# A wide layer's third quarter of weights decoded later, and the memory of the change lent to expert weights: attention, soft experts and a wide layer on one core

## The chip, the cores and the metric

The kernel runs on one core of a Trainium2 chip. TensorE (PE) multiplies matrices, VectorE (DVE) and ScalarE (ACT) work on the rest, GpSimd (POOL) has a few additions, and SyncE (SP) only issues transfers between device memory and the core's memory. The metric is the time of one execution on the device in microseconds (us).

## The reference

Three stages follow one another: a thresholded softmax attention, a layer of soft experts, and a wide layer. x has 2304 rows of 512.

```
scores = q @ k.T / sqrt(64)                       # 4 batches, 8 heads, 576 x 576
scores = where(scores >= rowmax(scores) - tau, scores, -1e9)
x = (softmax(scores) @ v)                         # heads side by side: 2304 x 512

logits = x @ phi                                  # 32 slots, 4 for each of 8 experts
slot_input = softmax(logits, over tokens).T @ x   # 32 x 512
slot_out[e] = relu(slot_input[e] @ w1[e]) @ w2[e] # w1 512x1024, w2 1024x512
x = softmax(logits, over slots) @ slot_out        # 2304 x 512

h = x @ w_in                                      # w_in 512 x 2048, in float64
out = (h * sigmoid(1.702 * h)) @ w_out            # w_out 2048 x 512, in float64
```

## The kernel before

**Attention** runs in 16 units (4 batches by 4 pairs of heads) of 9 tiles each. The order of the instructions is written out: a table PLAN gives each step a place within the 9 tiles of a unit, the steps of all units are sorted by these keys, and while they are issued `InOrder.on` keeps each engine's instructions in the order in which they stand in the program.

**Decoding.** w_in and w_out come as float64, that is as two 32-bit words per number. A piece is loaded as `raw` (SP, line 147), and the helper at line 134 records its work: ACT makes `y<-raw`; DVE makes `y<-y`, `top<-raw,y`, `y<-top`, `y<-raw,y`. For w_in one POOL addition of top and y gives the weights in f32. For w_out ACT casts top to `wo_h`, and DVE makes `top<-top,wo_h` and `wo_l<-top,y`, so that the weights are kept as a high and a low part. The buffers raw, y and top are each 3 deep in the wide layer (2 in attention).

The first WA columns of w_in are decoded in attention, in pieces of 128 x 256 (24 of them before: two in each of units 0 to 11) into the tiles `wi`. The columns behind WA are decoded in the wide layer, in pieces of 128 x 512 called "late" (4 before). The list `stream` of the wide layer has 9 pieces of w_out, the late pieces, then 7 of w_out.

**Experts.** w1 and w2 of 8 experts make 64 quarters of 512 KB. They are loaded into rings of buffers (a, b, c, ...), each of which takes memory that another use has left; some are loaded slowly in attention (`slow_load`), the others after it. Layer 1 is at line 1034, layer 2 at line 1076; a buffer of ring m, a or b is filled again as soon as an expert's work on it is over.

**Wide layer.** After the experts, slots times w_in gives `ws` (32 slots by 2048 hiddens, in pieces a, b, c, d of 384 or 512 columns behind a first one of 128). Since a sum of 4 products of 32 rows is taken side by side, a piece goes through PE (`w_ps`, line 1207), a copy to memory on ACT (`wqs`, line 1212), PE again (`w_ps<-wqs,sel`, line 1215), and from there into ws on ACT and DVE. Then 48 steps follow: 3 groups of 6 token tiles by 8 blocks of 128 hiddens, for the first half of the hiddens, and the same for the second half. A step makes `h_ps` (line 1249) in a part of 512 and one of 256 tokens, `sg` and `gh` on ACT (lines 1254, 1236), `gw` on DVE (line 1238), and 18 products `y_ps` (lines 1275 to 1277) with the weights of the step's hiddens. Sums of the first half are parked in memory (`part`, line 1285). Beside a step goes, in the first 5 steps and in the odd ones after them, the decoding of the next piece of the stream. SEQ and TAIL give the places of the pieces of ws: c is made at steps 4 and 5, d at 18 and 19 (the first of each pair is w_ps and wqs, the second the rest). In PSUM, the w_ps of a late piece of ws takes the one buffer, tag h0, in which the h_ps of 512 tokens is made too. In this stage Tile's scheduler sets the order on each engine from the program's order and from what depends on what; each engine works through its own list in order.

Of the kernel before, what the change touches and what calls it, by code (L numbers as in the profile page):

```python
# [19 lines left out]
def kernel(  # L20
# [14 lines left out]
    nc = tc.nc  # L35
# [19 lines left out]
    WA = 1536  # L55
# [3 lines left out]
    SEQ, TAIL, LATE = "wabhwawbhh", {4: "c", 5: "c", 18: "d", 19: "d"}, 9  # L59
# [15 lines left out]
    wi = [ring_a.tile([P, 2, WA], F32, tag="wi", name=f"wi{i}", bufs=2) for i in range(2)]  # L75


    order = [(1, 0), (1, 1), (1, 2), (2, 0), (1, 3), (2, 1)] + [(1, e) for e in range(4, E)]
    order += [(2, e) for e in range(2, E)]
    quarters = [(layer, e, j) for layer, e in order for j in range(4)]  # L80
    rings, ring_ctx, w_rows = {"a": ring_a}, {}, {}
# [3 lines left out]
    def load_quarters(ring, n, spread=False):  # L85
# [3 lines left out]
        while i < n and quarters:  # L89
# [8 lines left out]
            if spread:  # L98
                slow.append(io)
            else:  # L100
                nc.sync.dma_start(**io)
# [42 lines left out]
    first = [True]  # L144

    def load(**io):
        ins = nc.sync.dma_start(**io)  # L147
        if first[0]:
            tc.keep_in_program_order(ins)
# [42 lines left out]
    def w_in_piece(pool, j):  # L192
# [4 lines left out]
                out=wi[kc // 2][:, kc % 2, cols], in0=top, in1=rest  # L197
# [21 lines left out]
    def late_piece(pool, j, wl):  # L219
        n, kc = divmod(j, KC)  # L220
        cols = slice(n * DM, (n + 1) * DM)
        return decoding(
            pool, ("late", j), DM,
            lambda top, rest: po.tensor_add(out=wl[kc // 2][:, kc % 2, cols], in0=top, in1=rest),
# [20 lines left out]
    def attention():  # L245
# [3 lines left out]
        def psum(name, bufs):  # L249
# [3 lines left out]
        st, rows, sums, late_p2, early_p2, exp_e, odd_units, even_units, loads, weights_in = (  # L253
            ExitStack() for _ in range(10)
# [7 lines left out]
        pp = [pool(late_p2, f"pp{i}", 1, RIGHT) for i in range(2)]  # L262
        pp.append(pool(early_p2, "pp2", 1, RIGHT))
# [229 lines left out]
        def across(u, half):  # L493
# [8 lines left out]
            def after():  # L502
                row = l_row[u, half] = ptp.tile([P, 2 * P + R], F32, tag="l_row", name="l_row", bufs=2)
# [9 lines left out]
        def products_of(u, half):  # L513
            if (u, half) not in pt:
                n = 2 * P + half * R
                pt[u, half] = ptp.tile([P, 2, C, n], F32, tag=f"pt{half}", name="pt")
                ptr[u, half] = ptp.tile([P, n], F32, tag=f"ptr{half}", name="ptr")
# [365 lines left out]
        def unit(u):  # L883
# [49 lines left out]
            if u >= 4:  # L933
                for t in (7, 8):
# [39 lines left out]
        at(max(ends[f"DA{d}"] for d in range(2)) + 0.0001, swap, weights_in, "b", 4)  # L974
# [3 lines left out]
        freed("Q K R", floor, lambda: swap(loads, "c", 4))  # L978
        before = {n: TPU * (NU - 2) + max(PLAN[n][0:2]) for n in pairs.split()}
        floor[0] = max([floor[0]] + list(before.values())) + 0.0001  # L980
        at(floor[0], swap, even_units, "d", 2)
# [410 lines left out]
```

## Time and profile before

| | |
|---|---|
| time, median of 3 | 600.97 us (600.52 to 601.35) |
| profiled execution | 601.18 us, of which its span is 599.0 |
| PE | 582.7 us busy, 97% of the span |
| DVE | 400.5 us, 67% |
| ACT | 374.1 us, 62% |
| POOL | 140.9 us, 24% |
| bytes read from device memory | 64.55 MB |

Times of rows are from the start of the span. Attention lasts to about 320 us, the experts to about 363, the wide layer to the end. A busy share is an average over stages that have different limits. Where a row ends in square brackets, they hold the idle time of the engine just before it, and what ended it. Busy times of neighbouring instructions on one engine may overlap by some hundredths of a us.

### The profile page before, as it was taken

What the parts mean: (1) busy time and instruction counts of PE and PEld (TensorE: products, weight loads), DVE (VectorE), ACT (ScalarE), POOL (GpSimd) and SP (SyncE); (2) the same over time, 40 slices, a digit from 0 to 9 for tenths busy, and PEclk for the clock granted to TensorE, in tenths of its full rate; (3) what the DMA queues carried; (4) which work ended last, traced back from release to release, by engine and by line L of the source; (5) the groups of instructions that cost most, each with busy time, mean ns of one, the idle gap of its engine ahead of it and who ended that gap; (6) DMA issues with size and microseconds to landing.
All of it is one profiled execution on the core that took longest, in us unless ns stands there. A gap on an engine that the chain in (4) does not pass through costs nothing.

```text
span 599.0 us, 10535 instructions
## 1 busy us (share of the span) xinstructions
PE 582.7 (97%) x3712; PEld 414.1 (69%) x3712; DVE 400.5 (67%) x998; ACT 374.1 (62%) x804; POOL 140.9 (24%) x310
## 2 busy tenths in 40 slices
PE   7999999999999999999998998999999999999996
PEld 5666767667677676766765424778887788888884
DVE  3889899798997998878682435999981211512422
ACT  4788888788888798878861106767673354334330
POOL 1445445554455644222220100003000000000000
PEclk9899999999999999999999999999999999999999
DMA  7524054362542633420249993333310000200203
GB/s 223 136 74 124 21 161 144 88 180 92 161 143 62 172 125 80 138 75 24 87 150 369 410 409 144 134 120 130 138 37 0 1 0 1 105 1 0 106 0 106
DMA packets 63011, 69.94 MB, mean 117 GB/s; under 512 B 42736, under 2 KB 46832, under 8 KB 62960
## 3 DMA queue, kind: packets, MB, share of 16 engines
q1 hardware_dynamic: 62960, 69.28, 35.6%
q8 instruction: 29, 0.48, 0.3%
q14 instruction: 22, 0.18, 0.1%
HBM read 64.55 MB, written 4.72 MB: 116 GB/s over the span
## 4 chain that ended last, share of the span: by engine, by line
PE 87%; DVE 5%; DMA 3%; ACT 1%; SPq 1%; issue 1%; POOL 0%; DVEq 0%; POOLq 0%; ACTq 0%
PE s_ps L134 13%; PE o_ps L134 13%; PE y_ps L1275 11%; PE y_ps L1277 11%; PE y_ps L1276 11%; PE pt_ps L134 10%; PE r_ps L134 4%; PE h_ps L1249 3%; DVE p L134 3%; DMA w_c<-in_moe_w_dram 2%; PE acc L1034 2%; PE q_t L134 1%; SPq L147 1%; PE x_ps L134 1%; PE lg_ps L134 1%
## 5 line engine op out<-in xcount | busy, mean ns | idle before, releaser
L134 DVE SCALAR_TENSOR_TENSOR p<-p,th,e_sb 128x576 f32<-128x576 f32 x144 | 118.0, 841 | 13.5 <-ACT e_sb L134 11.4
L134 ACT ACTIVATE e_sb<-p,mn 128x576 f32<-128x576 f32 x144 | 110.7, 781 | 21.2 <-DVE p L134 20.3
L1275 PE MATMUL y_ps<-wo_h,gh 128*128 128x512 f32 x288 | 113.8, 396 | 0.0
L1276 PE MATMUL y_ps<-wo_l,gh 128*128 128x512 f32 x288 | 113.5, 394 | 0.0
L1277 PE MATMUL y_ps<-wo_h,gw 128*128 128x512 f32 x288 | 113.3, 395 | 0.0
L1238 DVE TENSOR_TENSOR gw<-sg,gh 128x768 fp32r<-128x768 f32 (+2 forms) x49 | 45.9, 939 | 91.9 <-ACT gh L1236 91.7
L134 DVE TENSOR_SCALAR_CACHE_REDUCE p<-s_ps 128x576 f32<-128x576 f32 x120 | 87.1, 751 | 10.3 <-PE pt_ps L134 6.6
L134 ACT COPY pt<-pt_ps 128x512 f32<-128x512 f32 x142 | 82.2, 586 | 17.8 <-PE pt_ps L134 17.1
L1254 ACT ACTIVATE sg<-h_ps 128x512 f32<-128x512 f32 (+1 forms) x96 | 42.5, 491 | 78.4 <-PE h_ps L1249 78.4
L134 PE MATMUL pt_ps<-ident,p 128*128 128x128 f32 x580 | 88.3, 280 | 0.5 <-DVE p L134 0.3
L134 PE MATMUL s_ps<-kx,qx 64*128 64x288 f32 x512 | 86.1, 438 | 2.2 <-DVE p L134 1.7
L134 PEld LDWEIGHTS pt_ps<-ident,p 128*128 128x128 f32 x580 | 65.3, 142 | 23.8 <-ACT ptr L134 5.4
L134 PE MATMUL o_ps<-pt,vn 128*64 128x320 f32 (+1 forms) x512 | 69.6, 412 | 0.3 <-ACT pt L134 0.3
L134 PEld LDWEIGHTS s_ps<-kx,qx 64*128 64x128 f32 x512 | 47.6, 189 | 25.0 <-issue 7.0
L1275 PEld LDWEIGHTS y_ps<-wo_h,gh 128*128 128x128 f32 x288 | 53.9, 187 | 14.1 <-ACT gh L1236 0.8
L1277 PEld LDWEIGHTS y_ps<-wo_h,gw 128*128 128x128 f32 x288 | 53.8, 187 | 13.5 <-DVE gw L1238 0.2
L1276 PEld LDWEIGHTS y_ps<-wo_l,gh 128*128 128x128 f32 x288 | 54.0, 187 | 11.2
L134 PEld LDWEIGHTS o_ps<-pt,vn 128*64 128x64 f32 x512 | 33.7, 136 | 31.0 <-issue 10.6
L134 POOL TENSOR_TENSOR th<-mn,few 128x1 f32<-128x1 f32 x144 | 38.7, 278 | 68.3 <-DVE p L134 63.4
L1236 ACT CAST gh<-sg 128x768 fp32r<-128x768 f32 (+2 forms) x49 | 40.2, 823 | 1.2
L134 POOL COPY lw<-l 128x256 f32<-128x256 f32 (+1 forms) x48 | 21.7, 472 | 34.8 <-PE r_ps L134 17.2
L134 ACT ACTIVATE y<-raw 128x256 f32<-128x256 f32 (+1 forms) x44 | 24.3, 551 | 8.9 <-DMA raw<-in_moe_w_out_dram 6.5
(189 smaller groups left out, 743.3 us busy)
## 6 DMA issues: line engine op xcount, KB each, us to landing
raw<-in_moe_w_out_dram SPq DMA_DIRECT2D x16, 512.0 KB, 3.3
raw<-in_moe_w_in_dram SPq DMA_DIRECT2D x24, 256.0 KB, 2.9
w_a<-in_moe_w_dram SPq DMA_DIRECT2D x12, 512.0 KB, 4.4
w_a<-in_moe_w_dram SPq DMA_DIRECT2D x6, 1024.0 KB, 13.8
qn<-in_q_dram SPq DMA_DIRECT2D x16, 256.0 KB, 3.7
kn<-in_k_dram SPq DMA_DIRECT2D x16, 256.0 KB, 4.0
vn<-in_v_dram SPq DMA_DIRECT2D x16, 256.0 KB, 2.9
w_m<-in_moe_w_dram SPq DMA_DIRECT2D x6, 512.0 KB, 5.0
```

The costliest lines, as they stand in the source:

```text
L134: ins = call(*args, **kw)
L147: ins = nc.sync.dma_start(**io)
L1034: nc.tensor.matmul(acc1[j][kc * NS:(kc + 1) * NS, :], s_in[kc // 2][:, kc % 2, e * NS:(e + 1) * NS], w_rows[1, e, kc][:, j * 512:(j + 1) * ...
L1236: nc.scalar.copy(out=gh[:, a], in_=sg[:, a])
L1238: nc.vector.tensor_sub(out=gw[:, a], in0=sg[:, a], in1=gh[:, a].bitcast(F32))
L1249: nc.tensor.matmul(ps, ws[:, f * P:(f + 1) * P], cs[:, t:t + n, :].rearrange("p t n -> p (t n)"), start=True, stop=True,)
L1254: nc.scalar.activation(out=part, in_=ps, func=AF.Gelu_apprx_sigmoid)
L1275: nc.tensor.matmul(ys[t], gh[:, tk], w_h, start=first, stop=False)
L1276: nc.tensor.matmul(ys[t], gh[:, tk], w_l, start=False, stop=False)
L1277: nc.tensor.matmul(ys[t], gw[:, tk], w_h, start=False, stop=last)
```

## The change

WA falls from 1536 to 1024. Pieces of w_in decoded in attention become 16 (units 0 to 7), late pieces 8. The tile wi takes 16 KB of a partition where two took 24, and what is left becomes two more buffers of ring c. The four quarters of ring c were one load of 2 MB; now six are loaded slowly, within units 9 and 10. The transposed weights of a unit's first half move from the pool ptp into one of their own, ptp0, which is given to ring p (2 quarters) before the last second half is over. Ring n (1 quarter) takes the memory of the loads of Q and K. Rings d and i hold one quarter less. Loads in attention are now chained to each other in the order of the table. From unit 3 on three slow loads stand in a unit, where two stood from unit 4 on. In layer 2 ring m is filled again, ring c no longer. In the wide layer piece c of ws moves from steps 4 and 5 to 13 and 14, d to 19 and 20, and steps 8, 12, 16 and 20 carry a piece of the stream where they had none. The parked sums of the first half lie in wi, ring m and ring k.

```diff
     PW = 256
-    WA = 1536
+    WA = 1024
     ES = NS + SE
     QSCALE = 1.0 / float(D) ** 0.5
     IN_ORDER = True
-    SEQ, TAIL, LATE = "wabhwawbhh", {4: "c", 5: "c", 18: "d", 19: "d"}, 9
+    SEQ, TAIL, LATE = "wabhwawbhh", {13: "c", 14: "c", 19: "d", 20: "d"}, 9
+    EXTRA = (8, 12, 16, 20)
     AHEAD = 3
...
     y_acc = const.tile([P, DM], F32, name="y_acc")
-    wi = [ring_a.tile([P, 2, WA], F32, tag="wi", name=f"wi{i}", bufs=2) for i in range(2)]
-
-
-    order = [(1, 0), (1, 1), (1, 2), (2, 0), (1, 3), (2, 1)] + [(1, e) for e in range(4, E)]
-    order += [(2, e) for e in range(2, E)]
+    wi = ring_a.tile([P, KC, WA], F32, tag="wi", name="wi", bufs=1)
+
+
+    order = [(1, 0), (1, 1), (1, 2), (2, 0), (1, 3), (2, 1), (2, 2)] + [(1, e) for e in range(4, E)]
+    order += [(2, e) for e in range(3, E)]
     quarters = [(layer, e, j) for layer, e in order for j in range(4)]
+    later_half = [(2, 2, 2), (2, 2, 3)]
+    at_k = quarters.index((2, 3, 0)) - 2
+    quarters = [x for x in quarters if x not in later_half]
+    quarters[at_k:at_k] = later_half
     rings, ring_ctx, w_rows = {"a": ring_a}, {}, {}
...
             else:
-                nc.sync.dma_start(**io)
+                load(**io)
             for x in range(m):
...
-    first = [True]
+    first, newest = [True], [None]
     def load(**io):
-        ins = nc.sync.dma_start(**io)
+        ins = nc.sync.dma_start(**io).ins
         if first[0]:
-            tc.keep_in_program_order(ins)
+            if newest[0]:
+                tc.add_manual_dep(
+                    ins, newest[0], mybir.DependencyInfo(
+                        mybir.DependencyClass.NoSync, mybir.DependencyReason.DATA
+                    ), reason="loads in the order of the table",
+                )
+            newest[0] = ins.name
...
             pool, ("in", j), PW, lambda top, rest: po.tensor_add(
-                out=wi[kc // 2][:, kc % 2, cols], in0=top, in1=rest
+                out=wi[:, kc, cols], in0=top, in1=rest
             ),
...
         pp = [pool(late_p2, f"pp{i}", 1, RIGHT) for i in range(2)]
+        ptps = [pool(half_0, "ptp0", 1, RIGHT), ptp]
         pp.append(pool(early_p2, "pp2", 1, RIGHT))
...
             def after():
-                row = l_row[u, half] = ptp.tile([P, 2 * P + R], F32, tag="l_row", name="l_row", bufs=2)
+                row = l_row[u, half] = ptps[half].tile(
+                    [P, 2 * P + half * R], F32, tag="l_row", name="l_row"
+                )
                 ac.copy(out=row[:, 0:2 * P], in_=ps[:, 0:2 * P])
...
                 n = 2 * P + half * R
-                pt[u, half] = ptp.tile([P, 2, C, n], F32, tag=f"pt{half}", name="pt")
-                ptr[u, half] = ptp.tile([P, n], F32, tag=f"ptr{half}", name="ptr")
+                pt[u, half] = ptps[half].tile([P, 2, C, n], F32, tag=f"pt{half}", name="pt")
+                ptr[u, half] = ptps[half].tile([P, n], F32, tag=f"ptr{half}", name="ptr")
...
                 batch(b, u)
-            if u >= 4:
-                for t in (7, 8):
+            if u >= 3:
+                for t in (2, 5, 8):
                     at(TPU * u + t + 0.9, slow_load)
...
-        at(max(ends[f"DA{d}"] for d in range(2)) + 0.0001, swap, weights_in, "b", 4)
+        decoded = max(ends[f"DA{d}"] for d in range(2)) + 0.0001
+        at(decoded, swap, weights_in, "b", 4)
+        at(decoded + 0.0001, add_ring, "c", 6, LEFT, True)
         tiles = range(TPU)
         pairs = " ".join(f"S{j}" for j in range(C)) + " L"
         floor = [0.0]
-        freed("Q K R", floor, lambda: swap(loads, "c", 4))
+        freed("Q K R", floor, lambda: swap(loads, "n", 1))
         before = {n: TPU * (NU - 2) + max(PLAN[n][0:2]) for n in pairs.split()}
         floor[0] = max([floor[0]] + list(before.values())) + 0.0001
-        at(floor[0], swap, even_units, "d", 2)
+        at(floor[0], swap, even_units, "d", 1)
         freed(pairs, floor, lambda: swap(odd_units, "e", 2))
         freed(" ".join(f"MK{t}" for t in tiles), floor, lambda: swap(exp_e, "f", 1))
         freed(" ".join(f"T{t}" for t in tiles), floor, lambda: swap(early_p2, "g", 1))
+        freed("A00 A01 A02 A03 LV0 LR0 VM0", floor, lambda: swap(half_0, "p", 2))
+
         def late():
             swap(late_p2, "h", 2)
             add_ring("lg", 0)
         freed("INV1 X0 X1 WD1", floor, late)
-        freed("A10 A11 A12 A13 LV1 LR1 VM1", floor, lambda: swap(sums, "i", 6))
+        freed("A10 A11 A12 A13 LV1 LR1 VM1", floor, lambda: swap(sums, "i", 5))
         rows_end = TPU * (NU - 1) + max(PLAN[n][2] for n in ("SS", "SSa", "XRS", "XR", "LN", "MS"))
...
                     )
-            if e < 2:
-                load_quarters("mc"[e], min(4, len(quarters)))
+            if e == 0:
+                load_quarters("m", min(4, len(quarters)))
...
+        def wl_at(n, kc, cols):
+            return held["wl"][2 * n + kc // 2][:, kc % 2, cols]
+
         def load_next():
...
-                        part_sums[g] = (
-                            rings["a"].tile([P, GT, DM], F32, tag="wi", name="part", bufs=2) if g < 2
-                            else spare_m[:, 0:3, :].rearrange("p a (b n) -> p (a b) n", n=DM)
-                        )
-                    nc.scalar.copy(out=part_sums[g][:, j, :], in_=ys.pop(t))
+                        part_sums[g] = True
+                        if g == 0:
+                            rows = rings["a"].tile([P, 8, DM], F32, tag="wi", name="part", bufs=1)
+                            parts.extend(rows[:, x, :] for x in range(8))
+                            parts.extend(spare_m[:, x, :] for x in range(8))
+                            parts.extend(spare_k[:, x, :] for x in range(2))
+                    nc.scalar.copy(out=parts[t], in_=ys.pop(t))
                 elif last:
-                    o = part_sums[g][:, j, :]
+                    o = parts[t]
                     nc.vector.tensor_add(out=o, in0=ys.pop(t), in1=o)
...
-        spare_m = rings["m"].tile([P, 4, F1], F32, tag="w", name="part_wl")
-        held["wl"] = [
-            spare_m[:, 3, :].rearrange("p (k n) -> p k n", k=2),
-            gp.tile([P, 2, DFF - WA], F32, name="wl", bufs=1),
-        ]
+        spare_m = rings["m"].tile([P, 8, DM], F32, tag="w", name="part_m")
+        spare_k = rings["k"].tile([P, 4, DM], F32, tag="w", name="part_k")
+        wl = gp.tile([P, 6, DM], F32, name="wl", bufs=1)
+        held["wl"] = [wl[:, 0:2], wl[:, 2:4], wl[:, 4:6], spare_k[:, 2:4]]
         held["gp"] = gp
...
-            now = i < FH - 3 or i % 2
+            now = i < FH - 3 or i % 2 or i in EXTRA
             w_steps = decode_next() if now else iter(())
```

On SP, at the start of the program, before (w_c is ring c, raw a piece of w_in):

```order
L147 DMA qkr<-in_q_dram 64x6x64
L147 DMA qkr<-in_k_dram 64x6x64
L101 DMA w_c<-in_moe_w_dram 128x4x1024
L147 DMA qn<-in_q_dram 128x8x64
L147 DMA kn<-in_k_dram 128x8x64
L147 DMA vn<-in_v_dram 128x2x256
L147 DMA v_left<-in_v_dram 64x64 x2
L147 DMA vn<-in_v_dram 128x2x256
L147 DMA raw<-in_moe_w_in_dram 128x512 x2
```

and after:

```order
L152 DMA qkr<-in_q_dram 64x6x64
L152 DMA qkr<-in_k_dram 64x6x64
L152 DMA qn<-in_q_dram 128x8x64
L152 DMA kn<-in_k_dram 128x8x64
L152 DMA vn<-in_v_dram 128x2x256
L152 DMA v_left<-in_v_dram 64x64 x2
L152 DMA vn<-in_v_dram 128x2x256
L152 DMA raw<-in_moe_w_in_dram 128x512 x2
```

The load of ring c has left the start; it stands in six parts in units 9 and 10.

On ACT, around the copy wqs of piece c in the wide layer, before (here numbers tell the buffers apart; raw is a loaded piece, y its first result):

```order
L1254 ACTIVATE sg_5117<-h_ps_5120 128x512
L1254 ACTIVATE sg_5117<-h_ps_5124 128x256
L134 ACTIVATE y_5135<-raw_5015 128x512
L1236 CAST gh_5118<-sg_5117 128x768
L134 CAST wo_h0_4835<-top_5095 128x512
L134 ACTIVATE y_5183<-raw_5056 128x512
L1212 COPY wqs_5163<-w_ps_5158 128x512
L1254 ACTIVATE sg_5165<-h_ps_5172 128x256
L1254 ACTIVATE sg_5165<-h_ps_5168 128x512
```

and after:

```order
L1274 ACTIVATE sg_5399<-h_ps_5402 128x512
L1274 ACTIVATE sg_5399<-h_ps_5406 128x256
L139 ACTIVATE y_5747<-raw_5587 128x512
L1256 CAST gh_5400<-sg_5399 128x768
L139 CAST wo_h1_4768<-top_5703 128x512
L139 ACTIVATE y_5817<-raw_5657 128x512
L1232 COPY wqs_5443<-w_ps_5438 128x512
L1274 ACTIVATE sg_5445<-h_ps_5452 128x256
L139 CAST wo_h1_4768<-top_5748 128x512
L1274 ACTIVATE sg_5445<-h_ps_5448 128x512
```

In both the `y<-raw` of a piece stands directly ahead of wqs. It is that of the 9th piece of the stream before, that of the 22nd after.

## Rows read from the trace of the kernel before

**Rows 1.** Busy time by stretch, wide layer: start:end length, PE PEld DVE ACT POOL, PEclk, DMA share, GB/s.
```profile
422.00:445.00 23.00, 23.00 (x103) 18.58 (x102) 23.00 (x42) 16.58 (x32) 0.00 (x0) 1.00 0.26 92
445.00:468.00 23.00, 23.00 (x103) 17.10 (x102) 6.22 (x8) 9.90 (x19) 0.00 (x0) 1.00 0.00 1
```

**Rows 2.** Groups on DVE, 365 to 447 us: count | busy us, mean ns | idle before.
```profile
L1238 DVE TENSOR_TENSOR gw<-sg,gh 128x768 fp32r<-128x768 f32 x17 | 16.1, 949 | 0.2
L134 DVE SCALAR_TENSOR_TENSOR top<-raw,y 128x512 uint32<-128x512 uint32 x20 | 15.7, 788 | 0.1
L134 DVE SCALAR_TENSOR_TENSOR y<-raw,y 128x512 f32<-128x512 uint32 x20 | 14.7, 733 | 0.1
L134 DVE TENSOR_TENSOR wo_l<-top,y 128x512 fp32r<-128x512 f32 x16 | 10.9, 682 | 0.0
L134 DVE TENSOR_TENSOR top<-top,wo_h 128x512 f32<-128x512 f32 x16 | 10.9, 682 | 0.0
L134 DVE TENSOR_SCALAR y<-top 128x512 uint32<-128x512 uint32 x20 | 9.3, 468 | 0.1
L134 DVE TENSOR_SCALAR y<-y 128x512 uint32<-128x512 uint32 x20 | 8.3, 417 | 0.1
```

**Rows 3.** Timeline of DVE: start us, us, instruction.
```profile
408.95 1.69 DVE L134 SCALAR_TENSOR_TENSOR y<-raw,y 128x512 f32<-128x512 uint32 x1
411.01 1.70 DVE L134 SCALAR_TENSOR_TENSOR top<-raw,y 128x512 uint32<-128x512 uint32 x1
418.83 1.40 DVE L134 TENSOR_SCALAR y<-top 128x512 uint32<-128x512 uint32 x1
...
445.17 0.69 DVE L134 TENSOR_TENSOR wo_l<-top,y 128x512 fp32r<-128x512 f32 x1
```

**Rows 4.** Timeline of POOL.
```profile
418.27 1.68 POOL L134 TENSOR_TENSOR wl<-top,y 128x512 f32<-128x512 f32 x1 [2.77 <-DVE y L134]
```

**Rows 5.** DMA issues (median us to landing), then timelines of PE and ACT.
```profile
raw<-in_moe_w_out_dram SPq DMA_DIRECT2D x16, 512.0 KB, 3.3
...
393.86 1.06 PE L1207 MATMUL w_ps<-wi,so_sb 128*32 128x512 f32 x8
...
436.74 0.51 PE L1249 MATMUL h_ps<-cs,ws 128*128 128x512 f32 x2
...
395.00 0.59 ACT L1212 COPY wqs<-w_ps 128x512 f32<-128x512 f32 x1
```

**Rows 6.** Experts' second layer: a stretch as in rows 1, then PE's timeline.
```profile
356.00:360.00 4.00, 3.71 (x28) 0.67 (x20) 0.00 (x0) 0.00 (x0) 0.00 (x0) 1.00 1.02 407
...
357.07 2.15 PE L1076 MATMUL acc<-w_m,h_in 128*32 128x512 f32 x12
359.44 1.05 PE L1076 MATMUL acc<-w_m,h_in 128*32 128x512 f32 x4 [0.23 <-DMA w_m<-in_moe_w_dram]
362.00 1.05 PE L1076 MATMUL acc<-w_c,h_in 128*32 128x512 f32 x4 [0.22 <-DMA w_c<-in_moe_w_dram]
```

**Rows 7.** Start of the program: timeline of SP's DMA issues, then of ACT.
```profile
6.29 0.61 SPq L101 DMA_DIRECT2D w_c<-in_moe_w_dram  x1
11.17 3.38 SPq L147 DMA_DIRECT2D vn<-in_v_dram  x1
16.47 0.94 SPq L147 DMA_DIRECT2D raw<-in_moe_w_in_dram  x2
...
20.05 0.44 ACT L134 ACTIVATE y<-raw 128x256 f32<-128x256 f32 x1 [1.93 <-DMA raw<-in_moe_w_in_dram]
```

**Rows 8.** PE's timeline, same matmuls of units 3, 6, 11 and 14 (counted from 0).
```profile
78.54 1.14 PE L134 MATMUL s_ps<-kx,q_left 128*128 128x288 f32 x4
...
135.38 1.14 PE L134 MATMUL s_ps<-kx,q_left 128*128 128x288 f32 x4
...
230.54 1.14 PE L134 MATMUL s_ps<-kx,q_left 128*128 128x288 f32 x4
...
286.53 1.14 PE L134 MATMUL s_ps<-kx,q_left 128*128 128x288 f32 x4
```

More of the change, by code (lines that the diff above doesn't have):

```diff
@@ L220, in late_piece @@
         n, kc = divmod(j, KC)
-        cols = slice(n * DM, (n + 1) * DM)
         return decoding(
             pool, ("late", j), DM,
-            lambda top, rest: po.tensor_add(out=wl[kc // 2][:, kc % 2, cols], in0=top, in1=rest),
+            lambda top, rest: po.tensor_add(out=wl(n, kc, slice(0, DM)), in0=top, in1=rest),
         )
@@ L250, in psum @@
             return st.enter_context(tc.tile_pool(name=name, bufs=bufs, space=PSUM))
-        st, rows, sums, late_p2, early_p2, exp_e, odd_units, even_units, loads, weights_in = (
-            ExitStack() for _ in range(10)
+        st, rows, sums, late_p2, half_0, early_p2, exp_e, odd_units, even_units, loads, weights_in = (
+            ExitStack() for _ in range(11)
         )
@@ L1048, in experts @@
                 load_quarters("aaab"[e], 4)
-        for name in ("md", "j", "i", "lg", "h", "g", "f", "e", "d"):
+        for name in ("md", "j", "i", "lg", "h", "p", "g", "f", "e", "d", "n"):
             ring_ctx[name].close()
@@ L1154, in decode_next @@
             if kind == "late":
-                return late_piece(mp, j, held["wl"])
+                return late_piece(mp, j, wl_at)
             h = j // 8 * 2
@@ L1187, in w_at @@
             if c0 >= WA:
-                return held["wl"][kc // 2][:, kc % 2, c0 - WA:c0 - WA + n]
-            return wi[kc // 2][:, kc % 2, c0:c0 + n]
+                return wl_at((c0 - WA) // DM, kc, slice((c0 - WA) % DM, (c0 - WA) % DM + n))
+            return wi[:, kc, c0:c0 + n]
         def slots_in(c0, n, bank):
@@ L1229, in ffn @@
         ]
-        part_sums = {}
+        part_sums, parts = {}, []
         gl, ys = {}, {}
```

## The prediction

> **What bounds the kernel now.** The page names PE, 97% busy, and the chain of work that ended last runs through PE for most of the span; but what a change is worth is read by stage. I read the wide layer first, by stretches. PE is busy for all of it there, and no wait of PE is listed after 370 us. But DVE is just as full: 23.00 of 23 us up to 445, then 6 of 23 [rows 1]. So from the start of the wide layer to about 446 us two engines are saturated side by side: PE with the steps, DVE with the decoding of 20 pieces and 17 steps' gw [rows 2]. PE doesn't feel it, since it uses the pieces later than DVE makes them. In the experts' second layer the transfers are the limit: the share of DMA is 1.02 at 407 GB/s, and PE waits for each quarter [rows 6]. At the start, ACT waits 1.93 us for the first raw of w_in [rows 7]. In attention the engines take turns, and a piece's decoding there is to be read from whole units [rows 8].
>
> **The change, part by part.**
>
> *Start.* The load of 2 MB stands ahead of the second part of Q, K, V and the first raw on SP at 6.29. Behind it one issue takes 3.38 us where others take 0.6, and raw is issued at 16.47 only, so ACT's y comes 1.93 us late, with exp, and so DVE and PE, behind it [rows 7]. Without it raw should land before ACT asks. PE can gain at most those 1.93 us, and at least nothing if another wait ends as late. I take 1.1, since ACT's wait is passed on in part.
>
> *Attention.* Units 8 to 11 lose their two pieces each. From unit 3 to unit 6 (all with decoding) the same matmuls stand 56.84 us apart, from 11 to 14 (none) 55.99 [rows 8]: 0.28 per unit. Four units are 1.1; since units differ in the slow loads as well, I take 0.9, between 0 and 1.6. Units 3 to 15 get more slow loads, 512 KB each, beside transfers that take a small part of the time; I cost them at nothing, as the raw and Q of the next unit are issued far ahead. If that cover is gone, a late Q costs what raw cost at the start, some 2 us.
>
> *Experts.* More quarters are in memory before layer 1: 22 of them (11 MB) stood to be loaded after it begins, 19 (9.5 MB) do now. One takes 1.28 us (359.44 to 362.00 for two, [rows 6]), so the last lands 3.8 us earlier: this is the upper bound. PE then has to be quick enough. From 357.07 its last 24 products cost, at four in 1.05 and eight more in 1.10 [rows 6], 1.05 + 20 x 0.1375 = 3.8, so they would end at 360.9 and not at 363.05: 2.2 less. Between 2.2 and 3.8 I take 2.6. Against it stand new waits of the experts for rings that come free in another order (first casts on DVE behind ring j), bounded by one or two quarters, 0 to 2.5; I take them as inside the 2.6.
>
> *Wide layer: the pieces.* Four more late pieces. On DVE each is y<-y 0.42, top 0.68, y 0.42, y 0.68, the means of [rows 2] without the longer ones told below (y<-raw: 14.7 less one of 1.69, over 19): 2.2 us, less 0.08 each where neighbours overlap, 1.9. And each late piece has a POOL addition. There were four, and beside each one DVE instruction is longer: 1.69 and 1.70 where its kind takes 0.68, 1.40 where it takes 0.42 [rows 3], and a second top<-raw; the one of 1.40 lies across POOL's 418.27 to 419.95 [rows 4]. That is 1.01 for y<-raw, 0.98 for y<-top, and 2.1 for the two top<-raw (15.7 less 20 x 0.68, [rows 2]): 4.1 us, 1.03 for each addition. So DVE gets 4 x (1.9 + 1.03) = 11.7 us more and is full until some 458 instead of 446. The weights of the second half are used from step 24 on, at about 483 us, so for y_ps alone this is free.
>
> *Wide layer: piece c.* It isn't free for piece c of ws. The order of ACT has the y<-raw of the 22nd piece directly ahead of c's wqs, where the 9th stood before. And w_ps of c holds the one h0 buffer, so the next h_ps of 512 tokens on PE waits for wqs; behind that h_ps stand all other products. When is the 22nd raw there? Its buffer is that of the 19th piece, free after DVE's y<-raw of that one, and the transfer takes 3.3 us [rows 5]. Before, DVE ended its last piece with wo_l, 445.17 + 0.69 less the overlap, at 445.8 [rows 3], having done the groups of [rows 2]: 20 of each of the four decoding steps, 16 top<-top, 16 wo_l and 17 gw. At the 19th piece's y<-raw it has, after the change, done 20 y<-y, 19 of the other three, 10 top<-top, 10 wo_l, 14 gw, and ws of c not yet: 0.68 + 0.42 + 0.68 + 6 x 0.68 + 6 x 0.68 + 3 x 0.95 + 0.7 = 13.5, less 19 x 0.08, is 12.0 less, and 4 more additions delay it by 4.1. That gives 445.8 - 12.0 + 4.1 = 437.9. Raw lands at 441.2, y and wqs take about 0.6 each (0.59 for wqs, [rows 5]): 442.4.
>
> PE's h_ps at that place ran at 436.74 [rows 5]. It comes earlier by what c took at steps 4 and 5, 1.06 for w_ps and about 0.9 for the product behind it, and then has c's 1.06 and the 1.0 of h_ps and three products ahead of the one that waits: 436.7 - 1.9 + 2.1 = 436.9. PE waits 5.5 us. Behind it gw must pass a DVE that is still full, for which I add 0.5: **6.0 lost**. Each 0.1 us on an addition's delay moves the 8 of them by 0.8. With no delay at all DVE would be there 8 us sooner and PE wouldn't wait; with 1.3 it would wait 8. Piece d, at step 19, comes at about 465, after the stream has ended: nothing.
>
> The Trainium skill ("SBUF — State Buffer", Who interferes with whom) says that DVE and GpSimd share one pair of ports as an exclusive lock for a whole instruction, and that issue order decides who is blocked. The rows show DVE blocked each time, for 1.0 us. By that rule POOL waits where DVE issues first; DVE would then lose nothing, and the time would be that of the first rival below, 596.4. Were DVE shut out for all of an addition of 1.68 us [rows 4], the loss would be some 11 (8 x 0.65 more).
>
> *EXTRA, memory of parked sums, copies of l_row:* the same instructions at other places, on engines with room (ACT 16.6 of 23 us, POOL none, [rows 1]); nothing.
>
> **Sum.** 601.18 + 6.0 - 2.6 - 1.1 - 0.9 = 602.6 for the profiled execution (span 599.0, and 2.2 around it). That execution is 0.2 above the median, so **602.4**.
>
> **Rivals.**
> *DVE keeps up, and PE doesn't wait in the wide layer.* Place: the additions fall into stretches where DVE waits for gh, or POOL is the one that waits. For it: DVE has 0.1 us of idle per group at most [rows 2], but nothing shows that all eight additions meet a DVE instruction of the sort. Against it: four of four did. It decides from 0.3 us per addition downwards (8 x 0.73 = 5.8 gained). Then 601.2 - 4.6 - 0.2 = **596.4**, faster. Up to a wait of 3.4 it is still faster.
> *Wait and gains cancel.* With 0.8 per addition the wait is 4 to 4.5: **600.6**, no change.
> *The gains before the wide layer aren't there.* The experts wait for rings that come free later, or slow loads delay raw and Q: 602.4 + 2.6 = **605.0**; with only half of it, 603.7.
> *The transfer is hidden anyway:* the start yields nothing as exp waits for something else: 603.5, within the forecast.
>
> **Numbers.** The forecast (a wait of 5 to 8 us, gains of 3.5 to 5) has 0.42, 600.9 to 605; a fifth of it lies under 602.2. DVE keeps up 0.22, cancelling 0.18, lost gains 0.18. A measurement of this kernel can tell 0.2% (1.2 us) from no change, so faster is under 599.8, slower above 602.2. Faster: 0.22 and 0.04 of the cancelling case; same: 0.14 and 0.08 of the forecast; slower: 0.34 and 0.18. The range from 596.2 to 606 leaves out a larger gain of the experts (3.8) without any wait, and a lock for a whole addition.
>
> **What would show it.** Right: PE has one wait of 5 to 7 us near 433 to 440 us at an h_ps, released by ACT's wqs, with y<-raw of ACT waiting for a raw; eight additions on POOL with a longer DVE instruction beside each; DVE full to nearly 460; DMA's full stretch before the wide layer some 3 us shorter; w_c no longer at 6.29 and no 1.93 us on ACT at 20. Wrong: no wait of PE in the wide layer; new waits of layer 1 or 2 for DVE's casts; units 3 to 11 longer by waits for Q or raw.

## The result, and the profile after

The changed kernel takes 608.47 us (median of 4, 604.73 to 609.79) against 600.97: ratio 1.0115, 95% interval 1.007 to 1.016. It is slower, as forecast, but by 7.5 us where 1.4 were forecast, and outside the range. The profiled execution is the shortest of the four: 604.73, span 602.6, mean clock 0.988. The other three have spans of 606.5 to 607.9 at a mean clock of 0.977 to 0.980. Span times mean clock is 595.4 for the first and 593.9 to 594.4 for the others: what sets them apart is the clock. Before it was 599.0 x 0.992 = 594.2. So there are two things to explain: in the profiled execution the gains of 4.9 us ahead of the wide layer are more than lost again in it, and the clock costs some us, in the other three executions more than in the profiled one.

**Ahead of the wide layer the terms hold.** The start, in the lists of SP and ACT:

```profile
10.43 0.94 SPq L152 DMA_DIRECT2D raw<-in_moe_w_in_dram  x2
...
17.64 0.77 ACT L139 ACTIVATE y<-raw 128x256 f32<-128x256 f32 x2
```

The first raw is issued at 10.43 (16.47 before, [rows 7]), and ACT's y<-raw follows without a wait. Units, by the same matmuls as [rows 8]:

```profile
76.65 1.14 PE L139 MATMUL s_ps<-kx,q_left 128*128 128x288 f32 x4
...
133.47 0.90 PE L139 MATMUL s_ps<-kx,q_left 128*128 128x288 f32 x3
...
228.04 1.14 PE L139 MATMUL s_ps<-kx,q_left 128*128 128x288 f32 x4
...
283.57 0.65 PE L139 MATMUL s_ps<-kx,q_left 128*128 128x288 f32 x2
```

Unit 3 stands 1.89 us earlier than before, unit 6 1.91, unit 11 2.50, unit 14 2.96. So the start gave 1.9 (I had 1.1, with 1.93 as its bound), and from unit 6 to unit 14, where units 8 to 11 have lost their decoding, another 1.05 came (I had 0.9). No loss by the extra slow loads shows up to there. The first w_ps of the wide layer, before and then after:

```profile
366.51 0.85 PE L1207 MATMUL w_ps<-wi,so_sb 128*32 128x384 f32 x8 [0.68 <-DVE ws L1182]
```

```profile
356.70 1.46 PE L1093 MATMUL acc<-w_m,h_in 128*32 128x512 f32 x10
361.64 0.85 PE L1227 MATMUL w_ps<-wi,so_sb 128*32 128x384 f32 x7 [0.68 <-DVE ws L1202]
```

That is 4.87 us earlier, and the last products of layer 2 (356.70) no longer wait for a transfer. Of the 2.96, 0.34 is lost in the last unit and its row sums: the experts' first product (`si`) stands at 320.75, 323.37 before, 2.62 earlier. So the experts gave 2.25 (I had 2.6). Sum 4.9 where I had 4.6.

**In the wide layer PE waits.** From the start of its first w_ps to that of its last y_ps it took 226.15 us before and takes 234.34. The waits of PE after 366 us (in total, times, longest):

```profile
PE h_ps L1269 <- ACT wqs L1232: 3.9, 1, 3.9
PE h_ps L1269 <- ACT sg L1274: 2.0, 2, 1.7
```

PE's timeline there, and ACT's:

```profile
427.72 0.66 PE L1269 MATMUL h_ps<-cs,ws 128*128 128x512 f32 x2 [1.75 <-ACT sg L1274]
438.63 0.79 PE L1269 MATMUL h_ps<-cs,ws 128*128 128x512 f32 x1 [3.93 <-ACT wqs L1232]
```

```profile
426.50 0.68 ACT L139 ACTIVATE y<-raw 128x512 f32<-128x512 f32 x1 [3.59 <-DMA raw<-in_moe_w_out_dram]
437.42 0.68 ACT L139 ACTIVATE y<-raw 128x512 f32<-128x512 f32 x1 [1.46 <-DMA raw<-in_moe_w_out_dram]
438.00 0.58 ACT L1232 COPY wqs<-w_ps 128x512 f32<-128x512 f32 x1
```

This is the wait that was forecast, to the instruction: PE stands at h_ps until 438.63 for wqs, wqs stands behind the y<-raw at 437.42, the 22nd, and that one waits for its raw. There is an earlier one of 1.75 that I had not seen, of the same make: sg behind the y<-raw at 426.50, which waited 3.59 for raw. Together (with a short one for sg) they are 5.9 us, where I had 6.0.

**And the clock falls behind it.** Stretches of 1 us, columns as in [rows 1], the granted clock third from the end:

```profile
437.00:438.00 1.00, 0.00 (x0) 0.00 (x0) 1.00 (x4) 0.58 (x2) 0.00 (x0) 1.00 0.00 0
438.00:439.00 1.00, 0.37 (x1) 0.37 (x2) 1.00 (x3) 0.86 (x3) 0.00 (x0) 0.54 0.00 0
440.00:441.00 1.00, 1.00 (x4) 0.73 (x3) 1.00 (x3) 0.97 (x2) 0.00 (x0) 0.50 0.62 242
441.00:442.00 1.00, 1.00 (x5) 0.81 (x4) 1.00 (x3) 0.94 (x2) 0.00 (x0) 0.75 0.00 0
442.00:443.00 1.00, 1.00 (x6) 0.81 (x5) 1.00 (x2) 0.01 (x1) 0.00 (x0) 1.00 0.62 209
```

PE did nothing from 434.7 to 438.6. From about 438 to 441.5 its clock is at 0.50, that is 1.2 GHz, and PE is busy for all but the first 0.6 us of it: the products behind the one at 438.63 start 0.43 us apart (439.22, 439.65, and so on to 441.35), where those from 441.66 on start 0.23 apart. This costs some 1.4 us. 5.9 of waits and 1.4 of clock are 7.3 of the 8.2 by which the wide layer grew; the other 0.9 is busy time of PE that I did not place. The sum had no term for the clock.

DVE is as forecast: full up to 445, and part of the time beyond:

```profile
422.00:445.00 23.00, 17.28 (x71) 12.06 (x70) 22.90 (x39) 11.90 (x22) 3.06 (x2) 0.93 0.39 137
445.00:468.00 23.00, 23.00 (x107) 18.06 (x105) 13.05 (x20) 13.56 (x26) 0.00 (x0) 1.00 0.00 1
```

### The profile page after: what moved, and what is told of

Read it like the earlier page. It is cut to its first block, busy times and chain, and to the rows that moved or that the text cites. A ratio compares the mean times of both kernels' runs of the same rounds, so it can differ in the third digit from the quotient of the medians.

```text
span 602.6 us, 10495 instructions
## 1 busy us (share of the span) xinstructions
PE 581.3 (96%) x3712; PEld 415.2 (69%) x3712; DVE 404.6 (67%) x990; ACT 374.7 (62%) x800; POOL 127.0 (21%) x290
## 4 chain that ended last, share of the span: by engine, by line
PE 84%; DVE 8%; issue 3%; ACT 2%; DMA 2%; SPq 0%; DVEq 0%; ACTq 0%
PE s_ps L139 14%; PE o_ps L139 13%; PE pt_ps L139 11%; PE y_ps L1295 9%; PE y_ps L1296 9%; PE y_ps L1297 9%; PE r_ps L139 3%; PE h_ps L1269 3%; PE acc L1093 3%; DVE p L139 2%; DVE y L139 2%; PE acc L1051 2%; PE q_t L139 1%; PE x_ps L139 1%; DVE top L139 1%
## 5 line engine op out<-in xcount | busy, mean ns | idle before, releaser
L1295 PEld LDWEIGHTS y_ps<-wo_h,gh 128*128 128x128 f32 x288 | 54.3, 189 | 14.1 <-ACT gh L1256 0.9
L1296 PEld LDWEIGHTS y_ps<-wo_l,gh 128*128 128x128 f32 x288 | 54.3, 189 | 11.2
L139 ACT ACTIVATE y<-raw 128x512 f32<-128x512 f32 (+1 forms) x40 | 23.4, 587 | 16.8 <-DMA raw<-in_moe_w_in_dram 10.6
L1269 PE MATMUL h_ps<-cs,ws 128*128 128x512 f32 (+1 forms) x96 | 27.3, 357 | 5.9 <-ACT wqs L1232 3.9
```

The costliest lines, as they stand in the source:

```text
L139: ins = call(*args, **kw)
L1269: nc.tensor.matmul(ps, ws[:, f * P:(f + 1) * P], cs[:, t:t + n, :].rearrange("p t n -> p (t n)"), start=True, stop=True,)
L1295: nc.tensor.matmul(ys[t], gh[:, tk], w_h, start=first, stop=False)
L1296: nc.tensor.matmul(ys[t], gh[:, tk], w_l, start=False, stop=False)
```

## The experiments

"Before" in the results is the kernel before, run on the same chip in the same session (601.4 to 602.2 us in all of them).

**The changed kernel again.**

> The changed kernel once more, for more executions with their clock. Theory (the two waits of PE in the wide layer make the granted clock fall, for longer in some executions than in others): times from 604.5 to 610, and span times mean clock near 595 in each, so the longer ones differ by clock alone; the profile shows a wait of 3 to 5 us on wqs and half clock behind it. Rival (the waits themselves differ from run to run by some 4 us, clock only follows): span times clock differs by as much as the span.

609.23 us (608.76 to 609.83), ratio 1.0123 (1.0103 to 1.0143). PE's timeline, and stretches of 10 us:

```profile
432.97 0.66 PE L1269 MATMUL h_ps<-cs,ws 128*128 128x512 f32 x2 [1.73 <-ACT sg L1274]
443.55 0.53 PE L1269 MATMUL h_ps<-cs,ws 128*128 128x512 f32 x1 [2.17 <-ACT wqs L1232]
...
320.00:330.00 10.00, 8.80 (x69) 4.60 (x72) 2.36 (x11) 1.14 (x5) 0.81 (x2) 0.83 1.04 415
360.00:370.00 10.00, 8.77 (x57) 4.01 (x50) 5.01 (x10) 4.99 (x12) 0.00 (x0) 0.83 0.17 55
430.00:440.00 10.00, 8.27 (x34) 5.57 (x32) 9.93 (x17) 6.16 (x11) 1.38 (x1) 0.83 0.42 145
440.00:450.00 10.00, 7.83 (x28) 5.43 (x25) 10.00 (x19) 4.71 (x9) 0.00 (x0) 0.83 0.46 157
```

The waits are shorter than in the first profile (1.73 and 2.17, where 3 to 5 were expected for wqs, with a few tenths more: 4.4 together), and yet the execution is 5.1 us longer. Behind the first 300 us the clock is low four times, for 3.4 us each: a mean of 0.83 in 10 us is 3.4 us at half, so 1.7 us lost each time. At 324 and 365, where the stage changes and both kernels have waits of 0.5 to 0.7 us, the first profiles showed no fall. At the start the clock is low from about 10 to 21 us, which loses 5.1 us, where it lost 3.4 in the first profiles of both kernels. Spans times clock are 593.6 to 596.6 in the four runs. So what differs between executions is the clock, as the theory has it, and the rival falls: it isn't the wait. That the two waits cause the low clock can hold for the falls at 433 and 444 only; the others stand ahead of them.

**Piece c late.** `TAIL = {19: "c", 20: "c", 23: "d", 24: "d"}`, all else as changed.

> The changed kernel with piece c of ws made at steps 19 and 20 and d at 23 and 24, where the stream has ended; nothing else is changed. Theory (the decoding is late, but costs time only because c's wqs stands behind it and PE behind wqs): the wait of 3.9 us is gone, up to 2 us of waits for sg remain, no long stretch at half clock, and the time is 597 to 600, below before, as the stages ahead of the wide layer gained 4.9. Rival (four more late pieces on a full DVE cost PE the time in any case, through sg, gh and gw): PE waits 5 us or more at other places, time 603 or more.

606.32 us (605.48 to 606.67), ratio 1.007 (1.0046 to 1.0093). The wait for wqs is gone, but the time lies above what was expected:

```profile
433.06 0.66 PE L1269 MATMUL h_ps<-cs,ws 128*128 128x512 f32 x2 [1.99 <-ACT sg L1274]
...
430.00:440.00 10.00, 8.02 (x29) 6.10 (x28) 9.93 (x17) 6.13 (x11) 1.38 (x1) 0.83 0.40 145
```

The wait for sg remains, 1.99, and the clock falls behind it. So c's place accounts for only some 3 of the 7.1 us by which after_again is behind before; moving it doesn't heal what stands behind the other y<-raw. Neither expectation is met: the waits, 2.3 together, are less than the gains ahead, and yet the kernel is slower than before, at a mean clock of 0.982 (before 0.990). Three of its four falls (at 10, 324 and 365 us) lie ahead of the wide layer.

**The additions on DVE.**

```diff
-            lambda top, rest: po.tensor_add(out=wl(n, kc, slice(0, DM)), in0=top, in1=rest),
+            lambda top, rest: ve.tensor_add(out=wl(n, kc, slice(0, DM)), in0=top, in1=rest),
```

> The changed kernel with the addition of each late piece on DVE instead of POOL. Theory (each POOL addition holds a DVE instruction up by about 1.03 us, more than the addition costs on DVE, 0.6): DVE is ready some 3 us sooner at piece c, the wait on wqs is 2 us or less, time 597 to 601; no DVE instruction of decoding is longer than its kind. Rival (POOL's addition costs DVE little, so that 8 more DVE instructions come on top): DVE is 3 to 5 us later, the wait grows to 7 or more, time 610 or more.

597.93 us (597.25 to 602.06), ratio 0.9948 (0.9925 to 0.9971): faster than before, and as expected. Groups on DVE, 360 to 462 us in the changed kernel and then 360 to 447 here, and what is left of PE's waits:

```profile
L139 DVE SCALAR_TENSOR_TENSOR top<-raw,y 128x512 uint32<-128x512 uint32 x24 | 18.5, 770 | 0.2
L139 DVE SCALAR_TENSOR_TENSOR y<-raw,y 128x512 f32<-128x512 uint32 x24 | 17.5, 730 | 0.2
L139 DVE TENSOR_SCALAR y<-y 128x512 uint32<-128x512 uint32 x24 | 12.4, 516 | 0.1
L139 DVE TENSOR_SCALAR y<-top 128x512 uint32<-128x512 uint32 x24 | 12.2, 507 | 0.3
```

```profile
L139 DVE SCALAR_TENSOR_TENSOR top<-raw,y 128x512 uint32<-128x512 uint32 x22 | 15.1, 686 | 0.0
L139 DVE TENSOR_SCALAR y<-y 128x512 uint32<-128x512 uint32 x23 | 9.7, 422 | 0.8 <-ACT y L139 0.7
L139 DVE TENSOR_TENSOR wl<-top,y 128x512 f32<-128x512 f32 x6 | 4.1, 684 | 0.0
...
PE h_ps L1269 <- DVE ws L1202: 0.8, 1, 0.8
```

Without POOL top<-raw is back at 0.686 from 0.770, y<-y at 0.422 from 0.516. The changed kernel's four decoding steps sum to 60.6 us for 24 pieces; at 0.686 and 0.422, twice each, they would be 53.2: 7.4 us for eight additions, 0.9 for each. POOL's own instructions are longer too: the eight take 12.4 us in the changed kernel, where most of those in late_from_5 (below) take 1.29 each, 10.3 for eight. But the edit did a second thing: ACT's list, which Tile's scheduler sets, came out otherwise: 20 y<-raw ahead of wqs, not 22. The next one takes this apart.

**The additions twice on DVE.** Each late piece makes its addition two times (the same values, work that isn't needed).

> As add_on_dve, with the addition of each late piece made twice on DVE (extra work; the result is the same), which costs DVE about 1.2 us per late piece, a little more than the 1.0 that POOL's addition cost it. Theory (what costs is DVE's time per late piece, whoever takes it): PE waits for ACT's sg and wqs are back, 3 us or more together, time 602 to 609. Rival (add_on_dve gained by another order of ACT's list, not by DVE's time): no waits over 1 us, time 597 to 600.

598.25 us (595.81 to 601.47), ratio 0.9923 (0.9891 to 0.9955). Here my theory fell. DVE is full (22.40 of 23 us) and PE doesn't wait at all:

```profile
422.00:445.00 23.00, 23.00 (x103) 17.26 (x102) 22.40 (x41) 15.66 (x30) 0.00 (x0) 1.00 0.39 128
```

Two additions on DVE (0.684 each) cost more of its time than POOL's one did (0.9), yet nothing is lost: the rival holds. ACT's list has 19 y<-raw ahead of wqs. What counts by this run is where the list puts them against DVE's real pace. That the list moves with additions on DVE (22, 20, 19 ahead) would fit a scheduler that counts these and not what an addition on POOL takes from DVE; how it reckons was not looked at.

**Both: additions on DVE, c at 19.**

> add_on_dve with piece c at steps 19 and 20 and d at 23 and 24. Theory: DVE keeps up and c is behind the stream, so the 0.8 us wait for ws goes too, no wait of PE in the wide layer, time 596 to 598. Rival (another wait takes its place, for sg behind y<-raw): as add_on_dve or above, 598 to 600.

598.92 us (596.24 to 601.55), ratio 0.9941 (0.9916 to 0.9967), no wait of PE behind the head of the wide layer: no better than add_on_dve by a margin that could be told.

**Only the place of c, in the kernel before.** `TAIL = {13: "c", 14: "c", 18: "d", 19: "d"}`.

> The kernel before with piece c of ws at steps 13 and 14 instead of 4 and 5, nothing else. In its ACT order 15 y<-raw of the stream stand ahead of c's wqs, not 22. Theory (the place of c costs only if wqs stands behind a raw that DVE hasn't let in yet): by step 13 those 15 are long done, no wait of PE over 0.5 us, time within 1 us of before. Rival (holding h0 for w_ps at that place costs PE by itself): a wait of 1 us or more at h_ps behind c, time 1.5 to 4 us above before.

614.39 us (611.98 to 616.13), ratio 1.0195 (1.0154 to 1.0236): both expectations missed. PE's timeline:

```profile
414.14 0.66 PE L1249 MATMUL h_ps<-cs,ws 128*128 128x512 f32 x2 [0.98 <-ACT sg L1254]
...
419.82 1.01 PE L1249 MATMUL h_ps<-cs,ws 128*128 128x512 f32 x2 [1.70 <-ACT sg L1254]
```

The scheduler took five pairs of h_ps out of their steps and put them in a row, one behind another, ahead of c; each waits for sg, since there is one buffer h0. PE has 4.9 us of waits for sg, and a clock of 0.85 and 0.64 in the two stretches of 10 us from 410 on. So this run doesn't price the place of c; it shows that a number in TAIL moves much else in the lists, and that one edit of this stage isn't one edit on the chip.

**The start alone, in the kernel before.** The loads chained as in the change, ring c's load through `load`.

> The kernel before with one edit: loads in attention are chained in the order of the table, so that the 2 MB load of ring c leaves the start (it goes to its place in the table). Theory (the first raw of w_in was late behind that load): ACT's wait of 1.93 us at 20 us is gone, units stand 1.9 us earlier from unit 1 on, time 1 to 2 us below before, 599.0 to 600.5 against 601 to 602. Rival (the load only moves and collides with others later, or the low clock at the start takes the gain): within 0.5 us of before.

600.34 us (597.33 to 601.29) against 602.03, ratio 0.9955 (0.9935 to 0.9975). ACT's y<-raw:

```profile
16.41 0.79 ACT L134 ACTIVATE y<-raw 128x256 f32<-128x256 f32 x2
```

ACT has no wait there, and the time is in the expected range. Not all of the 1.7 us need be that wait: the mean clock of these executions is 0.993 where before has 0.990, and the profiled one has no low clock at the start at all, so that its unit 3 stands 3.1 us earlier (75.44) and not 1.9. In the first profiles of the two kernels the clock at the start is alike, and there the difference is 1.9.

**Filling the wait.** 36 products of 256 columns on PE, ahead of the h_ps that waits:

```diff
                 next(pieces[TAIL[i]])
+                if i == 13:
+                    cover = ps_h.tile([P, 256], F32, tag="h4", name="cover")
+                    for _ in range(36):
+                        nc.tensor.matmul(
+                            cover, ws[:, 0:P], cs[:, 0:2, :].rearrange("p t n -> p (t n)"),
+                            start=True, stop=True,
+                        )
```

> The changed kernel with 36 products of 256 columns on PE behind w_ps of piece c, whose result nobody reads (extra work, to fill the wait for wqs). Theory (the wait costs twice, once as idle time and once by the clock that falls behind it): the wait stays in length, filled by some 4 us of products, the clock stays at 1.00 behind it, and the median falls to 602 to 605 with a mean clock of 0.987 or more. Rival (the low clock has another cause than the idle PE): the median stays at 607 to 610 at a mean clock of 0.98.

613.23 us (610.69 to 615.52), ratio 1.0188 (1.0153 to 1.0223). A miss as to time: the products run 4.6 us, and the wait that they cover was nearer 2 in these executions (2.2 in after_again, same chip); a new wait of 2.64 for c's ws came behind.

```profile
440.30 4.57 PE L1366 MATMUL cover<-cs,ws 128*128 128x256 f32 x36
455.24 0.50 PE L1269 MATMUL h_ps<-cs,ws 128*128 128x512 f32 x1 [2.64 <-DVE ws L1202]
...
440.00:450.00 10.00, 10.00 (x63) 8.47 (x59) 10.00 (x20) 5.52 (x10) 0.00 (x0) 1.00 0.47 159
```

One part can be read: with PE busy through that stretch the clock stays at 1.00 from 440 to 450, where after_again has 0.83. This is one execution and no proof, since the clock doesn't fall behind the wait of 2.64 either. Nor does the run tell the low clock's share in the median: the mean clock is 0.982, not the 0.987 or more that was expected.

**ACT's list against the additions, a set of four.** ACT's instructions of the wide layer are kept in the order of the program (`ac.activation(..., held=True)` for y, sg, gh, wo_h, wqs and the others). For "early" two pieces are begun in steps 5, 7, 9, 11 and 13, and one in each of the others of the first 14; for "dve" the addition is on DVE.

> The changed kernel with ACT's instructions of the wide layer kept in the order of the program, which puts 15 y<-raw of the stream ahead of c's wqs instead of 22; the additions stay on POOL. First of a set of four: 15 or 22 ahead, addition on POOL or DVE. Theory (what costs is that ACT's list runs ahead of what DVE can deliver; the scheduler set it without the time that POOL's additions take from DVE): with 15 ahead no wait of PE over 0.5 us though DVE is as slow as before, 596 to 600. Rival (DVE's lateness costs PE through sg and gw wherever c stands in the list): waits of 3 us or more remain, 603 or more.

> As late_list_pool_add (15 ahead), with the additions on DVE. Theory: no wait of PE over 0.5 us, time within 1 us of late_list_pool_add, since with room in ACT's list the price of POOL's additions isn't felt. Rival (DVE's time counts in itself): 3 us or more below late_list_pool_add.

> As late_list_pool_add, with pieces of the stream begun earlier in the program (each of the first 14 steps, two in steps 5, 7, 9, 11 and 13), so that 22 y<-raw stand ahead of c's wqs as in the changed kernel; ACT kept in that order, additions on POOL. Theory (the list against DVE's pace): waits for sg and wqs of 4 us or more together, half clock behind one of them, 604 to 612. Rival (it is the changed kernel's other edits, not the list): as late_list_pool_add within 1 us.

> As early_list_pool_add (22 ahead), with the additions on DVE. Theory (with the list fixed, each addition on POOL costs DVE about 1.0 us and on DVE 0.6): DVE is some 3 us sooner at the 19th piece, the waits are 2 to 4 us shorter than in early_list_pool_add, the time 2 to 6 below it. Rival (the port costs nothing; the whole gain of add_on_dve came from the scheduler's other list): no difference beyond 1 us, or slower.

607.23, 604.96, 613.43 and 612.02 us; ratios 1.0085 (1.0058 to 1.0111), 1.0054 (1.0035 to 1.0074), 1.0202 (1.0181 to 1.0224), 1.0155 (1.0109 to 1.02). All four have two new waits at the head of the wide layer, here of the first:

```profile
374.70 0.62 PE L1271 MATMUL h_ps<-cs,ws 128*128 128x512 f32 x2 [1.72 <-DVE ws L1204]
378.12 0.75 PE L1271 MATMUL h_ps<-cs,ws 128*128 128x512 f32 x2 [2.10 <-ACT sg L139]
```

and the low clock behind them, so that their times are not those of the place behind. Behind 380 us the late pair has no wait of PE over 0.2 us, with the additions on POOL as well; the early pair waits 1.9 and 2.4 for part, with POOL 1.4 for wqs and 1.3 for ws, with DVE 1.5 for part_m. So three more keep the order from step 5 on only:

```diff
         for i, s in enumerate(steps):
+            steady[0] = i >= 5        # held=steady[0] on ACT's instructions
```

> The changed kernel with ACT's instructions kept in the order of the program from step 5 of the wide layer on: 15 y<-raw ahead of c's wqs instead of 22, additions on POOL. Theory (ACT's list runs ahead of DVE's pace): no wait of PE over 0.5 us behind the head of the wide layer, 596 to 600. Rival (DVE's lateness costs PE wherever c stands): waits of 3 us or more, 603 or more.

> As late_from_5, with pieces begun earlier in the program, 22 y<-raw ahead of wqs, additions on POOL. Theory: waits of 2 us or more for part, sg or wqs between 410 and 455 us, half clock behind, 602 to 609. Rival (another edit of the change): within 1 us of late_from_5.

> As early_from_5, with the additions on DVE. Theory (with the list fixed, an addition costs DVE 1.0 us on POOL and 0.6 on DVE): the wait for wqs is 1 us or more shorter, the time 1 to 5 us below early_from_5. Rival (only the list counts): within 1 us of early_from_5.

late_from_5: 599.09 us (596.97 to 602.0), ratio 0.995 (0.992 to 0.9981). No wait of PE behind the head, with all eight additions on POOL, and DVE isn't even full any more:

```profile
399.00:422.00 23.00, 23.00 (x103) 18.58 (x102) 14.66 (x22) 13.84 (x27) 3.86 (x3) 1.00 0.36 112
422.00:445.00 23.00, 23.00 (x102) 17.06 (x102) 11.96 (x19) 10.76 (x21) 3.88 (x3) 1.00 0.22 68
...
434.80 0.59 ACT L139 COPY wqs<-w_ps 128x512 f32<-128x512 f32 x1 [3.10 <-PE w_ps L1230]
```

wqs is at 434.80, as soon as PE has made w_ps. In this kernel the additions on POOL hold DVE up hardly at all. Two of DVE's groups and one of POOL's, 360 to 520 us:

```profile
L139 DVE SCALAR_TENSOR_TENSOR top<-raw,y 128x512 uint32<-128x512 uint32 x24 | 17.5, 728 | 0.5
L139 DVE TENSOR_SCALAR y<-y 128x512 uint32<-128x512 uint32 x24 | 10.1, 420 | 0.2
L139 POOL TENSOR_TENSOR wl<-top,y 128x512 f32<-128x512 f32 x6 | 7.7, 1290 | 89.9 <-ACT part L139 69.3 <-DVE y L139 20.6
```

The four decoding steps sum to 54.3 us here, 1.1 above the 53.2 without POOL, where the changed kernel has 7.4. So the run does not show that DVE's delay by POOL is harmless: with this list most of that delay is gone as well.

early_from_5: 605.28 us (604.5 to 608.35), ratio 1.0069 (1.0039 to 1.01); early_from_5_dve: 605.24 us (602.33 to 606.75), ratio 1.0053 (1.0035 to 1.0071). Their waits, in that order:

```profile
PE y_ps L1298 <- ACT part L139: 3.7, 1, 3.7
PE h_ps L1272 <- DVE ws L1205: 1.6, 1, 1.6
PE h_ps L1272 <- ACT wqs L139: 0.9, 1, 0.9
```

```profile
PE y_ps L1298 <- ACT part L139: 3.4, 1, 3.4
PE h_ps L1272 <- DVE ws L1205: 0.6, 1, 0.6
PE y_ps L1298 <- ACT part_m L139: 0.4, 1, 0.4
```

late_from_5 and early_from_5 differ only in how early the pieces are begun, and by 6.2 us, as much as the waits of early_from_5 add up to: the list is the cause of the waits. (DVE's order differs along with ACT's, PE's hardly, so it is the list of both.) With ACT's list fixed, taking the additions off POOL removes the wait for wqs (0.9) and shortens that for ws by 1.0; the waits are 1.8 us less, but the medians are alike: the rival ("only the list counts") holds for the time. The greatest wait of the early pair, 3.4 to 3.7 for `part`, is of the same kind: a parked sum stands on ACT behind a y<-raw that came too soon.

## Why the prediction was wrong

- **The start, the attention and the experts** were right in mechanism and not far off in size: 1.9, 1.05 and 2.25 measured where the prediction had 1.1, 0.9 and 2.6. start_only shows the first by itself, mixed with the clock; the other two were read from the profile after, not tried alone.
- **The pieces.** "1.03 for each addition" measured 0.9 over eight. DVE's stretch reaches past 445 with 13 of 23 us busy, forecast was full to 458. The Trainium skill ("SBUF — State Buffer", Who interferes with whom) says that issue order decides who is blocked; the trace fits it in that both are held up, DVE by 7.4 us over the eight additions and POOL by 2.1 (12.4 for 10.3). The reading "DVE blocked each time" left POOL's part out: the 1.68 of [rows 4] is longer than the 1.29 of an addition that meets little. So the rival by which only POOL waits fell for the changed kernel. In late_from_5 DVE loses 1.1 over the eight: the price of an addition hangs on the list.
- **Piece c.** "PE waits 5.5 us", plus 0.5: 3.9 in the profiled execution, and 2.0 for sg behind another y<-raw. Sum 5.9, as forecast; in another execution 4.4. The place was right, the count of places one short, and that the sum fits is not all luck: less the 4.9 gained ahead, the prediction has wqs done at 437.5 and PE at its h_ps at 432.0; measured were 438.6 and 434.7. PE came later since it had already waited 2.0 for sg, for the same late DVE. No wait for gw is listed, so the 0.5 added for it shows in no run.
- **The step that failed** is the sum, "601.18 + 6.0 - 2.6 - 1.1 - 0.9", and the sentence that carries it to the median, "That execution is 0.2 above the median". Both take PE's clock as it was before. With the measured terms the sum gives 601.18 + 5.9 - 4.9 = 602.2; the profiled execution had 604.73. Of these 2.5 us, 1.4 are products at 1.2 GHz behind the wait for wqs. And this execution is not 0.2 above the median but 3.7 below it, at nearly the same span times clock: the step to the median was off by 3.9 us, by the clock. No rival had it.
- **How much of it is the clock.** On its chip the mean clock of after_again's four executions is 0.979, that of the twelve of before 0.990: over a span of 607.2 that is 6.7 of the 7.1 us between the medians. The waits that I had priced are paid for by the gains; the clock is the loss. In the profile of after_again 3.4 us of it stand behind the two waits of the wide layer. The rest stands ahead, at the start and at 324 and 365, and no run shows what it has to do with the change. add_on_dve and late_from_5, with next to no wait there, have the mean clock of before (0.990 and 0.989).
- **Not behind each wait.** Behind 400 us the profiles here have twelve waits of PE of 1.7 us or more. Around or behind nine of them the clock is low, for about 3.4 us or longer; behind three (1.75 in the first profile, 2.64 in cover_wait, 3.39 in early_from_5_dve) it stays at 1.00. early_from_5, with 6.2 us of waits, has a mean clock of 0.988 where before, run beside it, has 0.989: the 6.2 us by which it is behind late_from_5 are the waits.
- **What made DVE late** was argued too narrowly. "So DVE gets 11.7 us more" was near (four pieces more and 0.9 for each addition), but add_on_dve_twice, with some 11 us of additions on DVE, shows that this much doesn't hurt. What hurts is that ACT's list begins pieces sooner than DVE takes them, with instructions that PE needs standing behind in that list. The prediction read this from the order and priced it, but named the additions as the decider ("from 0.3 us per addition downwards"). The list is: 15 ahead 599.1, 22 ahead 605.3 with the additions on POOL, and 605.2 with them on DVE. The list also sets what an addition costs DVE (1.1 us in late_from_5 for all eight, 7.4 in the changed kernel).
- **Open:** why the changed kernel's clock falls also at 324 and 365 us, as in the profile of after_again, where the first profiles of both kernels show none. Both kernels have those waits. Kernels with next to no wait in the wide layer have such executions too (add_on_dve from 597.3 at 0.994 to 602.1 at 0.983; the profile of late_from_5 has both falls, at 323 and 364), so a part of the spread does not belong to the waits. Whether a fall in the wide layer makes another elsewhere more likely wasn't tried.

Three versions of the changed kernel without needless work beat both kernels: add_on_dve (0.9948), add_on_dve_c_at_19 (0.9941) and late_from_5 (0.995). Each keeps what the change saves ahead of the wide layer, and has next to no wait in it.

## What to carry to other kernels

Where a busy engine stands behind a list of another, look at what is directly ahead of the instruction that it needs, and when that one's input is there at the real pace. Here, holding ACT's list in the program's order from step 5 on, or moving the additions to DVE, which changed that list, turned a loss of 1.2% into a gain of 0.5%. What one engine takes from another belongs to the list too: the same eight additions cost DVE 7.4 us with one list and 1.1 with another. And a wait on a PE that is else full can cost more than its length: behind nine of twelve waits of 1.7 us or more the clock was low, which costs up to 1.7 us each time, so a forecast that rests on such a wait needs a term for the clock and a wider range.

## What the runs showed of the hardware

PE's granted clock fell to 0.50 for about 3.4 us around or behind waits of PE of 1.7 to 3.9 us, while PE was busy again, but not behind each: after the wait that ended at 427.72 in the first profile it stayed at 1.00, after its like at 432.97 in the second it fell, and after one of 3.39 in early_from_5_dve it stayed. It also fell at 324 and 365 us, behind waits of 0.5 to 0.7, in many of the profiles and not in the first ones. With 36 needless products in such a wait it stayed at 1.00, in one execution.

Additions on POOL lengthened DVE's instructions in the changed kernel by 0.9 us each, those with one input from memory (y<-y, 0.516 for 0.422 in the mean) too, and were themselves longer, 12.4 us for eight where 1.29 each is 10.3. In late_from_5, where DVE is 64% busy and less in the stretches from 399 to 445 us, they lengthened them by 1.1 us in all.
